# A 32-byte tile at SBUF's upper end in a retention and two-FFN kernel

## The chip, the cores and the metric

The kernel runs on one core of one Trainium2 chip. The metric is the device time of one execution in microseconds (us); the time of a kernel is the median of its runs. Times of single pieces come from one profiled execution.

## What is computed

A retention layer (linear attention with a decayed state) is followed by two feed-forward layers on 3072 tokens of width 512. All inputs are float32.

```python
# q, k, v: (4, 8, 768, 64)
state = gamma * state + k[t] (x) v[t]          # per head, 64 x 64
y[t] = scale * q[t] @ state
x = y as (3072, 512)
x = leaky_relu(x @ moe_w_in) @ moe_w_out       # 512 -> 2048 -> 512, slope 0.01
h = x @ moe2_w_in                              # 512 -> 2048
out = (h * sigmoid(1.702 * h)) @ moe2_w_out    # 2048 -> 512
```

## The kernel before

The work has three parts, and TensorE is the engine on which they follow each other.

**Numbers as two halves.** A float32 operand is split into a high part, rounded to TensorE's `float32r` type, and a low part, the remainder (`split`, lines 122 to 124). A product then takes three matmuls: high by low, high by high, low by high. So every large matmul here multiplies a stationary 128x128 block (the weights, `lhsT`) with a moving block of 128 rows and 512 or 384 columns (`rhs`), both of 4-byte numbers.

**First part: retention and the first FFN.** 24 steps of retention are interleaved with the first FFN. `ffn_in` (line 202) computes `h<-xs,home`: 12 matmuls of 512 columns for each of 16 slices of the hidden width and 6 blocks of 512 tokens. `ffn_out` (line 484) computes `y<-g,home`: 12 matmuls of 512 columns for each of the same slices. Weights come as 64-bit numbers and are converted by `work` on ScalarE, VectorE and GpSimd (lines 137 to 150) before their first use; those of `w_out` are converted while the first token block runs through `ffn_out`. Between them the weights of the second FFN are prepared (`Prep`).

**Second part: x times w_in of the second FFN.** `first` works in Strassen's scheme with 7 products (line 574): six matmuls of 384 columns for each product, `a`, `b` and `c<-xf,home`. The gated result goes to the DRAM tensor `gd`.

**Third part: times w_out of the second FFN.** `second` also has 7 products (line 757): matmuls of 512 columns, `d`, `e`, `f` and `h<-op,home`, in chains of 48. The blocks come back from `gd`, are combined (line 735) and split into `op` (lines 708 and 713). Line 769 transposes results with an identity matrix, `ident`.

**Where tiles lie.** Each tile belongs to a pool, and each pool grows from one of two sides of SBUF. The pools "left" are stacked upwards from the lower end, the pools "right" downwards from the upper end:

```python
pool = lambda c, name, bufs, side: c.enter_context(
    tc.tile_pool(name=name, bufs=bufs, side=side, reuse_waits="tile"))
homes = lambda n: pool(ctx, f"home{n}", 1, "left").tile([P, 4 * WQ], F32R, name=f"home{n}")
rest = {kind: pool(low, "rest" + kind, 1, "right").tile([P, 2048], F32R, name="rest" + kind) for kind in "io"}
g_p, h_p = pool(low, "g", 2, "right"), pool(low, "h", KF - 1, "right")
x_p, xs_p = pool(low_x, "x", 1, "right"), pool(low_x, "xs", 1, "right")
```

The lower side holds the weights of 14 of the 16 slices (`home0`, `home1`), the retention's tiles, and in the second part `xr`, `xt`, `xf`, `p`, `sg` and `g`. The upper side holds `resti` and `resto` (the weights of the last two slices of each matrix), `g`, `h`, `x`, `xs` and the conversion's `raw` and `a` in the first part, and in the third `op`, `ident`, `u` and the blocks of `gd`. In the built program the upper side's first tile, `resti`, begins at byte 221152 of a partition, and all other tiles of that side a multiple of 64 bytes below it: 221152 is 32 more than a multiple of 64. `home0` begins at 16512, `home1` at 73856 and the `xf` tiles at 146560 and so on, which are multiples of 64.

So the moving operands of lines 202, 484 and 757 (`xs`, `g`, `op`) begin 32 bytes past a multiple of 64, those of line 574 (`xf`) at a multiple; the stationary operands begin at a multiple except for `resti` and `resto`.

Of the kernel before, what the change touches and what calls it, by code (L numbers as in the profile page):

```python
# [9 lines left out]
F32 = mybir.dt.float32  # L10
# [9 lines left out]
P = 128  # L20
# [63 lines left out]
def retention_two_ffn(ctx: ExitStack, tc: tile.TileContext, qkv, consts, small, w1i, w1o, w2i, w2o, scratch, out):  # L84
# [5 lines left out]
    pool = lambda c, name, bufs, side: c.enter_context(  # L90
        tc.tile_pool(name=name, bufs=bufs, side=side, reuse_waits="tile"))
    homes = lambda n: pool(ctx, f"home{n}", 1, "left").tile([P, 4 * WQ], F32R, name=f"home{n}")
    low, low_x = ExitStack(), ExitStack()
    home = {"i": homes(0)}
    rest = {kind: pool(low, "rest" + kind, 1, "right").tile([P, 2048], F32R, name="rest" + kind) for kind in "io"}

# [433 lines left out]
    left, right = ExitStack(), ExitStack()  # L530
# [386 lines left out]
```

## Time and profile before

| what | value |
|---|---|
| median of the three runs shown | 1142.4 us |
| all three runs | 1141.04, 1142.4, 2821.34 us |
| the profiled execution | 1140.88 us |
| its span, first to last instruction | 1139.1 us |
| mean granted TensorE clock | 0.995 |
| TensorE's matmuls busy | 1115.6 us (98%) |
| VectorE busy | 694.6 us (61%) |
| ScalarE busy | 492.3 us (43%) |
| GpSimd busy | 269.1 us (24%) |
| DMA, mean over the span | 175 GB/s |

The busy time of an engine is the union of its instructions' times. Matmuls overlap: each takes some 400 ns from start to end, and the next starts about 233 ns after it, so the mean duration of one is not what it costs. What a matmul costs is the distance of two starts, read from a chain of them.

### The profile page before, as it was taken

The numbers are of one execution on the slowest core, as the hardware profiler recorded it, in microseconds if no ns is written. First come the engines' busy times: TensorE is split into PE (matmuls) and PEld (weight loads), VectorE is DVE, ScalarE is ACT, GpSimd is POOL, SyncE is SP. The second block draws the span as 40 slices with busy tenths as digits, with TensorE's granted clock in tenths as the row PEclk, the third lists the DMA queues.
The fourth block names the chain that finished last, engine by engine and source line by source line (L and its number), as shares of the span: only waits on it lengthen the run. The fifth ranks groups of instructions, "written<-read, shape, count | busy, mean of one in ns | idle before, by whom it ended". The sixth has DMA issues, their size and how long they took to land.

```text
span 1139.1 us, 16412 instructions
## 1 busy us (share of the span) xinstructions
PE 1115.6 (98%) x6188; PEld 939.2 (82%) x6189; DVE 694.6 (61%) x1034; ACT 492.3 (43%) x823; POOL 269.1 (24%) x269
## 2 busy tenths in 40 slices
PE   8999989999999999999999999999998999999997
PEld 5888867788888888888888899999998788888886
DVE  5977669645455546455442547575654686786774
ACT  2544445444344444344342434353432444545543
POOL 3655346422324233233321111111100000000000
PEclk9999989999999999999999999999999999999999
DMA  9888433225354445353449633436289625326322
GB/s 365 315 330 304 170 138 115 78 81 172 120 182 153 145 156 173 118 173 126 129 155 422 232 125 111 167 111 238 101 280 371 240 75 191 105 75 203 107 61 74
DMA packets 88095, 199.03 MB, mean 175 GB/s; under 512 B 7888, under 2 KB 51920, under 8 KB 82640
## 3 DMA queue, kind: packets, MB, share of 16 engines
q1 hardware_dynamic: 69584, 172.81, 43.6%
q10 hardware_dynamic: 18432, 25.17, 6.1%
q8 instruction: 48, 0.79, 0.3%
q14 instruction: 31, 0.25, 0.1%
HBM read 125.60 MB, written 72.35 MB: 174 GB/s over the span
## 4 chain that ended last, share of the span: by engine, by line
PE 92%; DMA 3%; DVE 2%; issue 1%; POOL 0%; ACT 0%; SPq 0%; ACTq 0%; POOLq 0%; DVEq 0%
PE h L202 23%; PE y L484 22%; PE b L574 9%; PE e L757 6%; PE d L757 6%; PE f L757 6%; PE a L574 6%; PE c L574 6%; PE h L757 3%; PE s L250 2%; PE o L287 2%; PE o L293 2%; DMA in<-qkv 1%; PE kv L281 1%; PE y L769 1%
## 5 line engine op out<-in xcount | busy, mean ns | idle before, releaser
L484 PE MATMUL y<-g,home 128*128 128x512 f32 x1008 | 250.0, 398 | 6.1 <-ACT home L123 3.7
L202 PE MATMUL h<-xs,home 128*128 128x512 f32 x1008 | 251.1, 397 | 0.0
L484 PEld LDWEIGHTS y<-g,home 128*128 128x128 f32 x1008 | 190.1, 189 | 54.5 <-POOL home L124 4.5
L202 PEld LDWEIGHTS h<-xs,home 128*128 128x128 f32 x1008 | 188.7, 188 | 47.4 <-issue 2.2
L124 DVE TENSOR_TENSOR g<-h,g 128x512 fp32r<-128x512 f32 x96 | 100.8, 1050 | 162.5 <-ACT g L123 162.5
L708 ACT CAST op<-g 128x512 fp32r<-128x512 f32 x168 | 100.9, 621 | 93.8 <-DVE g L735 42.1
L713 DVE TENSOR_TENSOR op<-g,op 128x512 fp32r<-128x512 f32 x168 | 112.1, 685 | 42.4 <-ACT op L708 39.8
L207 ACT ACTIVATE h<-h 128x512 f32<-128x512 f32 x96 | 57.3, 597 | 176.1 <-PE h L202 173.9
L574 PE MATMUL b<-xf,home 128*128 128x384 f32 x576 | 115.3, 334 | 1.2 <-DVE g L604 0.7
L574 PEld LDWEIGHTS b<-xf,home 128*128 128x128 f32 x576 | 101.1, 188 | 1.8 <-DVE g L604 1.0
L402 POOL TENSOR_TENSOR f<-f,raw 128x512 int32<-128x512 int32 x32 | 41.7, 1305 | 254.8 <-DVE f L398 254.8
L123 ACT CAST g<-h 128x512 fp32r<-128x512 f32 x96 | 59.7, 621 | 86.3 <-PE y L484 86.2
L574 PE MATMUL a<-xf,home 128*128 128x384 f32 x384 | 76.8, 334 | 0.0
L574 PE MATMUL c<-xf,home 128*128 128x384 f32 x384 | 76.8, 334 | 0.0
L757 PE MATMUL d<-op,home 128*128 128x512 f32 x288 | 70.3, 402 | 5.6 <-DVE op L713 5.6
L735 DVE TENSOR_TENSOR g<-g 128x512 f32<-128x512 f32 x96 | 72.1, 751 | 3.0 <-DMA g<-gd 3.0
L408 POOL TENSOR_TENSOR f<-f 128x128 f32<-128x128 f32 x128 | 71.9, 581 | 5.0
L757 PEld LDWEIGHTS d<-op,home 128*128 128x128 f32 x288 | 54.9, 192 | 19.2 <-DVE op L713 6.0
L757 PE MATMUL e<-op,home 128*128 128x512 f32 x288 | 70.2, 398 | 0.0
L757 PE MATMUL f<-op,home 128*128 128x512 f32 x288 | 68.2, 395 | 0.0
L574 PEld LDWEIGHTS a<-xf,home 128*128 128x128 f32 x384 | 67.5, 188 | 0.1
L574 PEld LDWEIGHTS c<-xf,home 128*128 128x128 f32 x384 | 67.5, 188 | 0.0
(94 smaller groups left out, 1396.7 us busy)
## 6 DMA issues: line engine op xcount, KB each, us to landing
gd<-g ACTq DMA_DIRECT2D x128, 192.0 KB, 2.0
g<-gd SPq DMA_DIRECT2D x96, 256.0 KB, 4.6
in<-qkv SPq DMA_DIRECT2D x21, 1024.0 KB, 7.1
home<-wdi SPq DMA_DIRECT2D x8, 1792.0 KB, 12.9
home<-wdo SPq DMA_DIRECT2D x8, 1792.0 KB, 9.6
raw<-w1i SPq DMA_DIRECT2D x16, 512.0 KB, 5.5
raw<-w1o SPq DMA_DIRECT2D x16, 512.0 KB, 3.3
raw<-w2i SPq DMA_DIRECT2D x32, 256.0 KB, 3.8
```

The lines of the kernel that those rows point to most:

```text
L123: nc.scalar.copy(out=hi, in_=src)
L124: (eng or nc.vector).tensor_tensor(out=lo, in0=src, in1=hi.bitcast(F32), op=ALU.subtract)
L202: nc.tensor.matmul(out=h, lhsT=w[:, a, k], rhs=xs[k][:, c], start=(i == 0), stop=(i == 3 * NP - 1))
L207: nc.scalar.activation(out=t, in_=h, func=AF.Lrelu)
L402: nc.gpsimd.tensor_tensor(out=self.f.bitcast(I32), in0=self.f.bitcast(I32), in1=self.low.bitcast(I32), op=ALU.add)
L408: nc.gpsimd.tensor_tensor(out=f[:, o], in0=f[:, a], in1=f[:, b], op=ALU.subtract)
L484: nc.tensor.matmul(out=y[j], lhsT=w[:, a, j * P : j * P + P], rhs=g[:, c], start=(m == 0 and i == 0), stop=(m == KF - 1 and i == 2))
L574: nc.tensor.matmul(out=t, lhsT=w[:, k, a], rhs=x[:, b, k], start=(start and m == 0), stop=(m == 5), skip_group_check=True)
L708: nc.scalar.copy(out=t[:, 0], in_=block_of(raw, *item))
L713: nc.vector.tensor_tensor(out=t[:, 1], in0=block_of(raw, *item), in1=t[:, 0].bitcast(F32), op=ALU.subtract)
L735: nc.vector.tensor_tensor(out=a(*s[0]), in0=a(*s[1]), in1=a(*s[2]), op=s[3])
L757: nc.tensor.matmul(out=t[:, j], lhsT=w[:, j, a], rhs=x[:, b], start=(new and q == 0 and m == 0), stop=(q == NQ - 1 and m == 2), skip_group ...
```

## The change

One line opens a pool of its own on the right, before all other pools of that side, with one tile of 8 float32 numbers (32 bytes in each partition). Nothing writes or reads it. It stays open to the end.

```diff
     low, low_x = ExitStack(), ExitStack()
+
+    pool(ctx, "pad", 1, "right").tile([P, 8], F32, name="pad")
     home = {"i": homes(0)}
     rest = {kind: pool(low, "rest" + kind, 1, "right").tile([P, 2048], F32R, name="rest" + kind) for kind in "io"}
```

In the built program each tile of the right side lies 32 bytes lower (`resti` at 221120, `xs` at 149440 for 149472, `op` at 225216 for 225248 and so on), at a multiple of 64. Tiles of the left side stay. The instructions of every engine, their order, their shapes and the semaphores that they wait for are the same as before; line numbers after line 93 are higher by two.

## Rows read from the trace of the kernel before

**Rows 1.** The page's first part: busy us of each engine, share, instructions.
```profile
PE 1115.6 (98%) x6188; PEld 939.2 (82%) x6189; DVE 694.6 (61%) x1034; ACT 492.3 (43%) x823; POOL 269.1 (24%) x269
```

**Rows 2.** Stretches: length, busy us by engine (instructions), granted TensorE clock, DMA share, GB/s.
```profile
30.00:143.00 113.00, 113.00 (x1300) 91.17 (x1297) 86.78 (x138) 50.95 (x88) 61.02 (x46) 1.00 0.78 279
149.40:153.70 4.30, 4.30 (x12) 3.33 (x11) 3.23 (x4) 1.98 (x5) 2.94 (x3) 0.50 0.39 122
157.00:205.00 48.00, 46.25 (x195) 36.02 (x194) 44.23 (x51) 28.20 (x48) 30.86 (x21) 1.00 0.33 108
215.00:645.00 430.00, 430.00 (x1851) 346.88 (x1850) 208.00 (x275) 179.52 (x284) 123.51 (x166) 1.00 0.48 166
650.00:873.00 223.00, 222.54 (x1284) 222.54 (x1285) 133.55 (x238) 88.17 (x176) 22.56 (x12) 1.00 0.52 182
889.00:1131.00 242.00, 242.00 (x1083) 195.35 (x1082) 176.55 (x266) 116.11 (x183) 8.18 (x3) 1.00 0.37 121
```

**Rows 3.** TensorE's longest waits: who waited for whom, us in total, times, longest.
```profile
PE d L757 <- DVE op L713: 5.6, 1, 5.6
PE y L484 <- ACT home L123: 3.7, 1, 3.7
PE y L484 <- POOL home L124: 2.4, 5, 0.6
```

**Rows 4.** The chain that ended last, from 299 us: start, us, engine, line, matmuls.
```profile
299.64 2.80 PE y L484 x12
302.44 2.80 PE h L202 x12
305.24 2.77 PE y L484 x12
308.00 2.80 PE h L202 x12
```

**Rows 5.** Groups of matmuls from 215 to 645 us: operands, shapes, count | busy, mean ns.
```profile
L484 PE MATMUL y<-g,home 128*128 128x512 f32 x840 | 206.0, 395 | 0.0
L202 PE MATMUL h<-xs,home 128*128 128x512 f32 x736 | 181.7, 395 | 0.0
L484 PE MATMUL y<-g,resto 128*128 128x512 f32 x144 | 34.9, 392 | 0.0
L202 PE MATMUL h<-xs,resti 128*128 128x512 f32 x120 | 29.3, 393 | 0.0
```

**Rows 6.** The chain that ended last, in the second part (384 columns).
```profile
661.32 1.04 PE c L574 x6
662.36 1.04 PE b L574 x6
```

**Rows 7.** The chain that ended last, in the third part (512 columns).
```profile
897.09 11.20 PE e L757 x48
908.29 11.20 PE f L757 x48
```

**Rows 8.** TensorE's instructions in order of time, 148 to 157 us: start, us, count.
```profile
148.80 4.63 PE L484 MATMUL y<-g,home 128*128 128x512 f32 x10 [0.61 <-POOL home L124]
153.24 3.73 PE L202 MATMUL h<-xs,home 128*128 128x512 f32 x12
```

**Rows 9.** Waits from 157 to 205 us: who waited for whom, us in total, times, longest.
```profile
PE y L484 <- POOL home L124: 1.8, 4, 0.5
```

**Rows 10.** Groups of VectorE and ScalarE: output<-input, shapes, count | busy, mean ns.
```profile
L713 DVE TENSOR_TENSOR op<-g,op 128x512 fp32r<-128x512 f32 x168 | 112.1, 685 | 42.4 <-ACT op L708 39.8 <-DMA g<-gd 1.4
L469 DVE TENSOR_TENSOR xf<-xr,xf 128x768 fp32r<-128x768 f32 x16 | 15.2, 952 | 2.8 <-ACT xf L468 2.4
L708 ACT CAST op<-g 128x512 fp32r<-128x512 f32 x168 | 100.9, 621 | 93.8 <-DVE g L735 42.1 <-PE f L757 15.6 <-PE e L757 13.3
L468 ACT CAST xf<-xr 128x768 fp32r<-128x768 f32 x16 | 13.3, 832 | 2.3 <-DMA xd<-y 2.3
```

**Rows 11.** The chain that ended last, at 1040 us: eight transposes.
```profile
1040.41 0.87 PE y L769 x8
```

## The prediction

> **What bounds the kernel now.** I read the busy times first: TensorE's matmuls fill 98% of the span, the next engine, VectorE, 61% [rows 1]. An average hides stages, so the stretches come next [rows 2]: from 215 to 645 us and from 889 to 1131 us TensorE is busy all the time, and no other engine above 73% there (VectorE, 176.55 of 242 us); from 157 to 205 us VectorE is at 44.23 of 48 us and TensorE is the one that now and then waits. Then the waits of TensorE: few and single, 5.6 us at the start of the third part, 3.7 us before the first `y` matmul, five of at most 0.6 us [rows 3]. So time can only come out of the matmuls themselves, and the question is what one of them costs by its start address, since the change alters nothing else.
>
> The chain of waits shows that cost as the distance of starts. A block of 12 matmuls of 512 columns with weights from `home0` or `home1` takes 2.80 us, 233.3 ns each [rows 4]; 48 in the third part take 11.20 us, again 233.3 ns [rows 7]. Six matmuls of 384 columns take 1.04 us, 173.3 ns each [rows 6]. The granted clock is 1.00 in all these stretches [rows 2], the level of 2.4 GHz, at which 512 columns take 213.3 ns and 384 take 160.0 ns at one column a cycle. What is over that is 20.0 ns for 512 columns and 13.3 ns for 384.
>
> Three things speak for the moving operand's start address as a part of it. First, the 384-column ones read tiles of the left side, at multiples of 64 bytes, and the 512-column ones read tiles 32 bytes off; the difference of the two excesses, 6.67 ns, is the time of 16 columns, which is 64 bytes of the moving stream. 2048 bytes that begin 32 bytes off a multiple of 64 touch 33 pieces of 64 bytes instead of 32; 1536 bytes that begin at a multiple touch just 24. Both stages then cost two pieces over the number touched. Second, the addresses of the weights matter: the block whose weights lie in `resto`, 32 bytes off like its moving operand, takes 2.77 us instead of 2.80 [rows 4], 230.8 ns each by the rounded row. Third, at half the clock the excess is gone: in 149.4 to 153.7 us, after a wait of 3.7 us for a converted weight [rows 3], the granted clock is 0.50 (1.2 GHz) [rows 2], and the matmuls there run at about one column a cycle: ten of them take 4.44 us from their first start to that of the next block [rows 8], 444 ns each with one delayed start among them, where 512 columns at 1.2 GHz take 426.7 ns. A cost of decoding or of the array would not vanish; a memory that delivers at a fixed rate, just short at 2.4 GHz, would behave so.
>
> **The change part by part.** The unused tile issues nothing: no instruction, no DMA, no wait, cost 0. All instructions, their order and what they wait for stay; 32 bytes of free space go. What is left is the address of each right-side tile.
>
> *Matmuls at lines 202, 484 and 757.* They would cost what the left-side form costs over its columns, 13.3 ns: 226.7 ns instead of 233.3, 6.67 ns less (233.3 - 226.7). The trace does not show an aligned operand of 512 columns, so the bounds: from above 233.3, as now (and 3 ns over it, see the rival on the slower side); from below 213.3, the bare column time. I take 226.7, the row with 4-byte operands at multiples of 64. By stretch:
> - 215 to 645 us: 840 + 736 = 1576 matmuls with `home` weights [rows 5], 1576 x 6.67 = 10.5 us. Those with `resto` and `resti`, 144 + 120 = 264, are at 2.77/12 = 230.8 ns now, 4.1 ns over 226.7: 264 x 4.1 = 1.1 us. VectorE has 208 of 430 us busy there, so nothing takes the place of the matmuls.
> - 889 to 1131 us: 1083 instructions less 88 transposes are 995 matmuls, x 6.67 = 6.6 us. VectorE at 176.55 of 242 us still fits in 235.
> - Before 143 us: 192 matmuls of line 202, 168 with `home` (x 6.67) and 24 with `resti` (x 4.1), 1.2 us. TensorE is busy throughout from 30 us, and the DMA engines are at 0.78 [rows 2], so loads can follow a stage that is 1% shorter. If they can't, this term is 0.
> - 149.4 to 157 us, at 1.2 GHz: 0, since no excess is seen there.
> - 157 to 205 us: TensorE waits four times for converted weights, 1.8 us in total [rows 9], with VectorE at 92%. A faster TensorE only waits longer, so its 195 matmuls (195 x 6.67 = 1.3 us) count as 0; if the conversion has slack after all, the 1.3 us come on top. The 44 matmuls or so of 205 to 215 us, without waits, give 0.3 us.
>
> *The second part, 650 to 873 us:* everything that its matmuls read is on the left side: 0.
>
> *Transposes (line 769):* eight take 0.87 us [rows 11], 109 ns each for 128 columns, twice the 53 ns of their columns, so the moving stream is not what they wait for. Their data move too; I count 0, with bounds of 6.67 ns either way for each of 96, 0.6 us.
>
> *VectorE, ScalarE, GpSimd.* Compare a right-side group with a left-side one of the same kind: VectorE's subtraction takes 685 ns for 512 columns on the right and 952 ns for 768 on the left [rows 10]. The 256 columns between them cost 267 ns, 1.04 ns a column, which leaves 685 - 533 = 152 and 952 - 800 = 152 ns. ScalarE: 621 and 832 ns, 0.82 ns a column, and 199 ns left over in both. No trace of the address: 0; and they lie beside TensorE except from 157 to 205 us. The DMAs into these tiles are the same in number and size; the one place where TensorE waits for their result, the 5.6 us at the start of the third part [rows 3], would have to shrink by a third to give 2 us, and I count 0.
>
> Sum: 10.5 + 1.1 + 6.6 + 1.2 + 0.3 = 19.7 us. The profiled execution took 1140.9 us (1139.1 in the span, 1.8 around it), 0.1% under the median of 1142.4, so I put the forecast against it: 1140.9 - 19.7 = 1121.2 us, 1.7% less. A difference of 2% is about what a measurement of this kernel can tell from no change, and this one stays just inside.
>
> A rule of the Trainium skill speaks against it. "SBUF — State Buffer", section "Door 1: The DMA port swizzle (why `[64,N]` ≈ `[32,N]`)", gives SBUF lines of 16 bytes, with a penalty where accesses cross to a new line. 32 is a multiple of 16, so by that rule the old addresses already begin on a line, both layouts touch the same number of lines, and the sum would be 0. The trace does not fit it well: the two kinds of block in [rows 4] differ only in whether the weights begin at a multiple of 64 or 32 past it, and take different times. A second rule, in "TensorE: Matmul & The Clock Gate", section "Step-by-step: what each phase is for", says that two independent read ports keep the next weights from slowing the running matmul; by that the 2.77 and the 2.80 us blocks would be equal, which they are not.
>
> **The rivals.**
>
> *Nothing happens (start addresses in steps of 32 bytes are free).* Mechanism: the moving stream is fetched in pieces of 32 bytes or fewer, of which it touches the same number before and after, and the 20.0 and 13.3 ns differ by the number of columns (for instance 6.67 ns for each 128 columns after the first). It is what the Trainium skill's rule of 16-byte lines on the page above would make of this kernel. For it: I have no row with equal columns and different alignment of the moving operand. Against it: the `resto` blocks, where an address of 32 bytes off moves the time. Time: 1141 us.
>
> *The excess goes with the columns, and alignment gives back a part.* 13.3 ns x 512/384 = 17.8 ns, 2.2 ns less than now, 2.2/6.67 of the sum: 6.5 us, 1134.4 us. For it: two points fit a line as well as a step. Against it: 2.2 ns is no multiple of anything seen.
>
> *More is gained.* If the left-side excess of 13.3 ns is due to the weights and the moving stream meeting unequally spread over the shorter matmul, a longer aligned stream may hide half of it: 6.67 ns more on some 2800 matmuls, 18.7 us, 1102.5 us. For it: excess vanishes at half the clock, so it is no fixed cost. Against it: 173.3 ns holds over the whole second part, with weights and moving operand both at multiples of 64.
>
> *Slower: the streams collide.* With weights and moving operand on the same grid of 64 bytes, each fetch of weights may fall on the fetch of the moving stream, as it cannot while the two are half a piece apart. Place: every matmul of lines 202, 484 and 757. Price: if what the `resto` blocks gain by their weights' address (233.3 - 230.8 = 2.5 ns) were lost instead, 3300 x 2.5 = 8 us, 1149 us; it decides from any distance above 233.3 ns. Against it: in `resto` blocks both are on the same grid and faster, and the same holds in the second part.
>
> **How the numbers follow.** The forecast, 1121.2 us with a range of its own from 1117 (the 1.3, the 0.6 and some of the waits come on top) to 1125 (the early stage and the `resto` share give nothing): 0.66. Nothing happens: 0.15. Part of it: 0.07. More: 0.08. Slower: 0.04. Outside 1116 to 1143 us lie most of the third and the last of the rivals, about 0.12. Faster by over 2% means under 1119 or so: the rival with more (0.08) and the lower end of the forecast (0.14), 0.22. Slower by over 2% needs 1165 us, 0.01. Within 2%: 0.77.
>
> **What would show it right or wrong.** In the chain of waits of the changed kernel, 12 matmuls of lines 204 and 486 would stand with 2.72 us, whatever their weights, and 48 of line 759 with 10.88 us; six of line 576 with 1.04 us as before. The stretch of 430 us would be 418 us long, the third part 6.6 us shorter, and the waits for converted weights around 157 to 205 us would each be some 0.2 us longer. Blocks of 2.80 us would refute the step on the matmuls outright; 2.77 us would say that only the agreement of weights and moving operand counts. If the blocks shrink but the span does not, a wait has opened that I did not see, and it would stand before a `y` matmul for `g` or before a `d` matmul for `op`.

## The result and the profile after

The changed kernel takes 1128.7 us in the median (1126.96 to 1129.34), 1141.8 us before; the ratio is 0.989 with a 95% interval of 0.9876 to 0.9904. One of the four runs before took 2821.34 us; the ratio leaves it out, and without it their median is 1141.2 us. The kernel is faster, and by less than 2%, as forecast. The size does not hold: 19.7 us less was forecast (1121.2 us), and the profiled execution went from 1140.88 to 1128.83 us, 12.05 us less. 1128.7 lies outside the forecast's own range of 1117 to 1125 us; it lies inside 1116 to 1143 us only because that range also covers the rivals, one of which is that nothing happens. A part of the mechanism must be wrong.

The page's first part of the changed kernel answers to [rows 1]: TensorE lost 12.3 us of busy time, the other engines changed by 1.8 us at most.

```profile
PE 1103.3 (98%) x6188; PEld 940.3 (83%) x6189; DVE 696.4 (62%) x1034; ACT 491.5 (44%) x823; POOL 269.8 (24%) x269
```

The chain that ended last in the changed kernel (start, us, engine, line, matmuls) answers to [rows 4, 6, 7]; lines are two higher.

```profile
299.97 2.75 PE h L204 x12
302.72 2.72 PE y L486 x12
...
660.98 1.04 PE b L576 x6
...
888.90 10.99 PE e L759 x48
```

Blocks with `home` weights fell from 2.80 to 2.75 us, chains of 48 from 11.20 to 10.99 us: 229.0 ns a matmul, not the 226.7 forecast. The block with `resto` weights (at 302.72) has the forecast's 2.72 us, 226.7 ns. The 384-column ones stay at 173.3 ns. So two kinds of block still differ although every start address of these matmuls is now a multiple of 64.

The stretches (columns as in [rows 2]) show that the rest is nearly as it was: the clock, VectorE's load, the DMA share, and half the clock after the wait before the first `y` matmul.

```profile
149.20:153.00 3.80, 3.80 (x10) 2.97 (x9) 3.22 (x4) 1.78 (x4) 2.44 (x3) 0.50 0.45 138
156.00:204.00 48.00, 45.59 (x195) 36.05 (x193) 45.06 (x51) 28.00 (x47) 31.74 (x21) 1.00 0.33 112
212.00:636.00 424.00, 424.00 (x1858) 348.62 (x1857) 210.65 (x276) 179.60 (x286) 125.72 (x167) 1.00 0.48 169
```

From 156 to 204 us the same 195 matmuls take the same 48 us with 0.66 us less busy time than in [rows 2]: the gain turned into waiting. TensorE's longest waits, to set beside [rows 3]:

```profile
PE d L759 <- DVE op L715: 5.7, 1, 5.7
PE y L486 <- ACT home L125: 3.8, 1, 3.8
PE y L486 <- POOL home L126: 2.7, 5, 0.7
PE b L576 <- DVE g L606: 1.4, 1, 1.4
```

The last of these waits was there before, too, but shorter:

```profile
PE b L574 <- DVE g L604: 0.7, 1, 0.7
```

The instructions and their order are the same in both kernels, so the start of one and the same matmul can be set side by side, which shows where the time went:

| start of the same matmul | before, us | after, us | us gained since the row above |
|---|---|---|---|
| `y`, the first of ten that run on, at half the clock | 148.80 | 148.62 | 0.18 (since the start) |
| `y` after the next `h` block, at the full clock | 156.80 | 156.03 | 0.59 |
| `y` after the last wait for a converted weight | 204.79 | 204.13 | -0.11 |
| the first of line 574 (576) | 643.23 | 634.42 | 8.15 |
| `d` after the wait at the start of the third part | 885.62 | 877.71 | -0.90 |
| the last group of transposes | 1132.91 | 1120.83 | 4.17 |

The 0.59 us in the second row are mostly a matter of the clock: before, the granted clock is still 0.50 from 154.0 to 154.6 us, and with the change it is 0.91 from 153.4 to 154.0 us. What brought it back some 1 us sooner is not shown.

### The profile page after: what moved, and what is told of

Same layout as the page of the kernel before. It is cut to its first block, busy times and chain, and to the rows that moved or that the text cites. A ratio compares the mean times of both kernels' runs of the same rounds, so it can differ in the third digit from the quotient of the medians.

```text
span 1127.0 us, 16412 instructions
## 1 busy us (share of the span) xinstructions
PE 1103.3 (98%) x6188; PEld 940.3 (83%) x6189; DVE 696.4 (62%) x1034; ACT 491.5 (44%) x823; POOL 269.8 (24%) x269
## 4 chain that ended last, share of the span: by engine, by line
PE 91%; DVE 4%; DMA 2%; issue 1%; ACT 1%; POOL 0%; SPq 0%; ACTq 0%; DVEq 0%; POOLq 0%
PE h L204 22%; PE y L486 22%; PE b L576 9%; PE a L576 6%; PE d L759 6%; PE f L759 6%; PE c L576 6%; PE e L759 5%; PE h L759 3%; PE s L252 2%; PE o L289 2%; PE o L295 2%; PE kv L283 1%; DMA home<-wdo 1%; DVE raw L141 1%
## 5 line engine op out<-in xcount | busy, mean ns | idle before, releaser
L486 PE MATMUL y<-g,home 128*128 128x512 f32 x1008 | 246.2, 395 | 6.5 <-ACT home L125 3.8
L204 PE MATMUL h<-xs,home 128*128 128x512 f32 x1008 | 246.5, 394 | 0.0
```

The lines of the kernel that those rows point to most:

```text
L204: nc.tensor.matmul(out=h, lhsT=w[:, a, k], rhs=xs[k][:, c], start=(i == 0), stop=(i == 3 * NP - 1))
L486: nc.tensor.matmul(out=y[j], lhsT=w[:, a, j * P : j * P + P], rhs=g[:, c], start=(m == 0 and i == 0), stop=(m == KF - 1 and i == 2))
```

## The experiments

**Three theories.** Only addresses changed, so the question is which property of them counts. *Theory G* is the prediction's: each operand by itself, whether it begins at a multiple of 64 bytes. *Theory M*: the moving operand's own start, modulo 128. *Theory D*: the distance of the moving operand from the weights, `moving - home`, modulo some period, whatever the two are by themselves. The last came from the blocks above: `resto` lies at the same place modulo 128 as `g`, and `home` does not. Addresses below are those of the built programs; a distance is given modulo 256 bytes, between `xs`, `g` or `op` and `home0` or `home1`. It was 96 before the change and is 64 with it. Between `xf` and the `home` weights it is 0 in both kernels, and so it is between `xs` and `resti` and between `g` and `resto`.

One thing fits no theory of a block's own distance: `resto` blocks have distance 0 in both kernels, and yet take 2.77 us before [rows 4] and 2.72 with the change. Inside such a block of the kernel before, the first seven matmuls take 1.62 us, 231 ns each, and then three take 0.68 us, 226.7 ns each:

```profile
305.24 1.62 PE y L484 x7
306.86 0.68 PE y L484 x3
```

So a block also depends on the one that ran before it. This comes back with the weights that are 16 bytes into their tiles.

**The tile of 96 bytes instead of 32 (right96), distance 0.**

```diff
-    pool(ctx, "pad", 1, "right").tile([P, 8], F32, name="pad")
+    pool(ctx, "pad", 1, "right").tile([P, 24], F32, name="pad")
```

> The unused tile has 96 bytes for 32: right-side tiles begin at multiples of 128 (the change: 64 past one), home weights at multiples of 128 as always. Theory D (the distance of moving operand and weights modulo 128 sets the cost, 0 is best): all 512-column matmuls at 226.7 ns, 12 of them in 2.72 us for 2.75 with the change, 48 in 10.88 us; 3024 x 2.28 = 6.9 us less than the change, about 1122 us. Theory M (the moving operand's own start modulo 128 sets it, 0 is best): the same. Theory G (only multiples of 64 count, for each operand by itself): 2.75 us stays, 1128.7 us.

Measured: 1122.76 us, ratio to the kernel before the change 0.9839 (0.9825 to 0.9854). Its chain:

```profile
297.52 2.72 PE h L204 x12
300.24 2.72 PE y L486 x12
...
665.13 1.04 PE c L576 x6
...
895.15 10.88 PE f L759 x48
```

All blocks are at 226.7 ns. Theory G alone has fallen: with all starts at multiples of 64, as with the change and here, there are still two speeds.

**Both sides 64 past a multiple of 128 (right32_left64), distance 0.**

```diff
     pool(ctx, "pad", 1, "right").tile([P, 8], F32, name="pad")
+    pool(ctx, "padl", 1, "left").tile([P, 16], F32, name="padl")
```

> The change, and an unused tile of 64 bytes at the lower end too: both sides begin 64 past a multiple of 128, so the distance is 0 and no start is at a multiple of 128. Theory D: 226.7 ns, 12 in 2.72 us, 48 in 10.88 us, six of 384 columns in 1.04 us as before, about 1122 us. Theory M: 229.0 ns as with the change, 12 in 2.75 us, and the 384-column matmuls slower than 173.3 ns by up to 2.3 ns, 1129 to 1132 us. Theory G: as the change, 1128.7 us.

Measured: 1122.31 us, ratio 0.9835 (0.9818 to 0.9851).

```profile
300.61 2.72 PE y L487 x12
...
665.14 1.04 PE c L577 x6
...
906.07 10.88 PE d L760 x48
```

The moving operands lie where they do with the change, and yet a block takes 2.72 us: theory M has fallen, and it is the weights' place beside theirs that did it.

**No operand of the large matmuls at a multiple of 64 (left96), distance 0.**

```diff
-    pool(ctx, "pad", 1, "right").tile([P, 8], F32, name="pad")
+    pool(ctx, "padl", 1, "left").tile([P, 24], F32, name="padl")
```

> No tile at the upper end but one of 96 bytes at the lower end: both sides begin 96 past a multiple of 128, so the distance is 0 and nothing is at a multiple of 64. Theory D: 226.7 ns, 12 in 2.72 us, 48 in 10.88 us, six of 384 columns in 1.04 us, about 1122 us. Theory M: 233.3 ns as before the change, and the 384-column matmuls some 5 ns slower, 1141 + 1344 x 5 ns = 1148 us. Theory G: 233.3 ns and 180 ns, 1141 + 1344 x 6.7 ns = 1150 us.

Measured: 1123.51 us, ratio 0.9842 (0.9827 to 0.9857).

```profile
298.00 2.72 PE h L204 x12
300.71 2.72 PE y L486 x12
...
665.96 1.04 PE c L576 x6
...
896.83 10.88 PE f L759 x48
```

This settles it against alignment. The right side is untouched, each moving operand of the first and third part begins 32 bytes off a multiple of 64 as before, `xf` and the weights do so now as well, and the whole gain is there, with 173.3 ns for 384 columns still. Of the three theories only the distance is left.

**A control (right64), distance 32.** The tile has 64 bytes (`[P, 16]`).

> A control: the unused tile at the upper end has 64 bytes, so right-side tiles begin 32 past a multiple of 128 (before the change: 96 past it), still 32 off a multiple of 64. Theory D: a distance of 32 for one of 96, both a quarter of the period off, so 233.3 ns, 12 in 2.80 us, 1141 us. Theories M and G: 233.3 ns too, 1141 us. If a shift of any size helps, the time falls as with the change to 1129 us.

Measured: 1140.8 us, ratio 0.9996 (0.9985 to 1.0007). A shift alone gives nothing: the chain shows `home` blocks as before, and `resto`, which still agrees with `g`, faster (2.73 us).

```profile
300.63 2.79 PE h L204 x12
303.43 2.73 PE y L486 x12
...
896.22 11.20 PE e L759 x48
```

**The period (right224), distance 128.** The tile has 224 bytes (`[P, 56]`), so that the right side begins at multiples of 128, of 256 even.

> The unused tile has 224 bytes: right-side tiles are again at multiples of 128, but the distance of moving operand and weights is 128 modulo 256, where with 96 bytes it is 0. Theory D with a period of 128 bytes: 226.7 ns, 12 in 2.72 us, 1122 to 1123 us as with 96 bytes. Theory D with a period of 256 or more: a distance of 128 costs something, as 64 does (229.0 ns, 12 in 2.75 us) or more, 1129 us or above.

Measured: 1138.93 us, ratio 0.9975 (0.9965 to 0.9985).

```profile
298.08 2.79 PE y L486 x12
300.87 2.78 PE h L204 x12
303.66 2.73 PE y L486 x12
...
895.04 11.16 PE e L759 x48
```

A period of 128 has fallen: at 128 a matmul costs 232.5 ns. Nor is the period 512: modulo 512 the three kernels of distance 0 are at 256 (`xs` less `home0`), while the `rest` tiles are at 0, and both reach 226.7 ns.

**The direction (right160), distance 192.** The tile has 160 bytes (`[P, 40]`).

> The unused tile has 160 bytes: the distance is -64 bytes (192 modulo 256) where the change has 64. If only the size of the distance counts: 229.0 ns, 12 in 2.75 us, 48 in 10.99 us, 1128 to 1129 us. If its direction counts (weights ahead of or behind the moving stream): another value between 226.7 and 233.4 ns, 1122 to 1141 us.

Measured: 1140.99 us, ratio 0.9995 (0.9986 to 1.0005).

```profile
298.55 2.80 PE y L486 x12
301.35 2.80 PE h L204 x12
304.14 2.75 PE y L486 x12
...
897.27 11.20 PE e L759 x48
```

A moving operand 64 bytes ahead of the weights modulo 256 cost 229.0 ns, 64 behind 233.3 ns: the direction counts. The `resto` block (at 304.14), at distance 0 as in every kernel so far, takes 2.75 us here, 2.73 in right64 and in the block shown of right224, 2.72 with the change and 2.77 before: its time goes with the blocks around it.

**Weights 16 bytes into their tiles (right96_home16).**

The tile of 96 bytes is there as in right96; to the kernel before, the edit is (some lines between are left out):

```diff
-    homes = lambda n: pool(ctx, f"home{n}", 1, "left").tile([P, 4 * WQ], F32R, name=f"home{n}")
+    homes = lambda n: pool(ctx, f"home{n}", 1, "left").tile([P, 4 * WQ + 32], F32R, name=f"home{n}")[:, 4 : 4 * WQ + 4]
...
+    pool(ctx, "pad", 1, "right").tile([P, 24], F32, name="pad")
```

> As with 96 bytes at the upper end, but the weights of home0 and home1 begin 16 bytes into their tiles, so the distance is 16 bytes for every matmul with home weights, the 384-column ones too, while resti and resto keep 0. Theory D has no value for 16: if any distance counts, between 226.7 (distance 0) and over 233.3 ns (32), 12 in 2.72 to 2.82 us, and the 384-column ones above 173.3 ns; if the grain is 32 bytes, 226.7 or 233.3 ns sharp. By the rule that 16-byte lines are all that counts, distance 32 could not have cost anything, and 16 would cost nothing either: 1122 us. My guess is about 230 ns, with 175 ns for 384 columns, 1122 + 3024 x 3.3 ns + 1344 x 2 ns = 1135 us.

Measured: 1129.78 us, ratio 0.9891 (0.9878 to 0.9905). The experiment is not quite the one announced: the larger `home0` pushes `home1` up by 128 bytes, so the distance is 240 with `home0` and 112 with `home1`. So it tries two other distances instead of 16; the guess of 1135 us was 5 us too high. What it showed was not expected by any theory. The chain around 214 us, where the first block of distance 0 after the waits for converted weights runs (`y` with `resto` weights), and pieces of the second and third part:

```profile
208.14 2.81 PE y L486 x12
210.95 2.80 PE h L204 x12
213.75 2.75 PE y L486 x12
216.49 2.72 PE h L204 x12
...
646.31 1.06 PE a L576 x6
...
676.75 1.04 PE b L576 x6
...
898.62 10.88 PE f L759 x48
...
948.50 8.16 PE h L759 x36
...
960.25 8.40 PE d L759 x36
...
979.86 11.20 PE f L759 x48
```

`h` blocks at 210.95 and 216.49 us are the same work at the same distance, 2.80 us before the `resto` block and 2.72 us after it, and it stays so to the end of the first part. (Two `resti` blocks of distance 0 had run earlier, among the retention's steps; after the waits that followed them, blocks took 2.80 us.) In the third part the first block of tokens runs at 10.88 us for 48, the second at 11.20, with the same two distances (half of each chain reads `home0`, half `home1`). So the distance does not set the cost by itself: there is a state that lasts from one matmul to the next. That it is a phase between the two streams which TensorE reads is an explanation and not shown; "phase" stands for it below. In the second part no such state is seen: blocks of 384 columns take 1.06 us (176.7 ns) where the weights come from `home0` and 1.04 us (173.3 ns) where they come from `home1`, all through.

**The same without a block of distance 0 in the first FFN (right96_all16).** `resti` and `resto` get the same 16 bytes (`[P, 2048 + 32]`, sliced from 4).

> As the kernel with weights 16 bytes into home0 and home1, but resti and resto are moved by 16 bytes too (their tiles grow by 128 bytes each), so that no block of the first FFN has a distance of 0: modulo 256 it is 240 with home0, 112 with home1, resti and resto. In the kernel before this one the first FFN went from 2.80 us a block to 2.72 us at the first resto block, whose distance was 0, and stayed there with the same home weights. Theory H (the streams keep the phase that they have; a block of distance 0 brings it in order, and a distance of 16 does not disturb it): without such a block 2.80 us stays to the end of the first part, and the time is about 1140 us. Theory D alone (the distance of a block sets its cost): the blocks with home weights are as there, 2.72 us from 214 us on, 1130 us.

In the built program `resto` is at 240 and only `home1` and `resti` at 112; no block of the first FFN is at 0, as intended.

Measured: 1142.77 us, ratio 1.0013 (1.0004 to 1.0023).

```profile
211.87 2.80 PE h L204 x12
214.67 2.80 PE y L486 x12
...
980.75 11.20 PE e L759 x48
...
1062.66 10.88 PE e L759 x48
```

Without that block 2.80 us stays to the end of the first part, as theory H says and theory D alone does not. The third part goes the other way round than in right96_home16: slow in its first two blocks of tokens, fast in the last. In both kernels each change of speed in the third part falls on a group of transposes or on a wait, where the run of 512-column matmuls is broken off (as between 948.50 and 960.25 us in the chain above). Why the speed is high after one of them and low after another was not found.

**Moving the retention's tiles as well (right96_smalls).** With the tile of 96 bytes, `smalls` is 24 numbers longer and the tiles behind it begin at multiples of 128.

> As with 96 bytes at the upper end, and the retention's smalls tile is 96 bytes longer, so that the tiles behind it (cst, st, sm, qs) begin at multiples of 128 like the tile in; before they are 32 off. Of the retention's matmuls only those of line 289 (weights sm, moving in, or the reverse) change their distance, from 32 to 0. Theory D: the 16 matmuls of a step there take less than 0.88 us, by at most 16 x 6.7 ns = 0.1 us, some 2 us in 24 steps, 1120 to 1122 us. If 128-column matmuls are not short of their moving stream, nothing: 1122.8 us.

Measured: 1124.3 us, ratio 0.9843 (0.9828 to 0.9858). The step's 16 matmuls, in the kernel before (line 287) and here (line 289):

```profile
24.98 0.88 PE o L287 x16
63.24 0.88 PE o L289 x16
```

They take 0.88 us as before, and the kernel is no faster than with the 96 bytes alone. But the expectation was written for a period of 128. Modulo 256, in the built program, the distance of these matmuls (`sm` from `in`) went from 32 to 128 and not to 0. So the run shows that this move gains them nothing; what distance 0 would do for matmuls of 128 columns is not shown.

**The change once more (change_again)**, on one chip with right224, right96_home16 and right96_smalls.

> The change itself, on the same chip as the others of this group. All theories: 12 matmuls with home weights in 2.75 us, with resto weights in 2.72 us, a time of 1127 to 1129 us, 5 to 7 us above the kernel with 224 bytes if the period is 128 bytes.

Measured: 1129.21 us, ratio 0.9886 (0.9871 to 0.9901).

```profile
299.02 2.75 PE h L204 x12
301.77 2.72 PE y L486 x12
...
889.98 10.99 PE e L759 x48
```

The block times are those of the first run of the change.

The kernels with one distance for all `home` weights together, with the cost of a 512-column matmul from the chains of 48 (us divided by 48); the two kernels with weights 16 bytes into their tiles have two distances and two speeds and are left out:

| distance modulo 256 | kernel | ns per matmul | median, us |
|---|---|---|---|
| 0 | right96, right32_left64, left96 | 226.7 | 1122.8, 1122.3, 1123.5 |
| 32 | right64 | 233.3 | 1140.8 |
| 64 | the change, change_again | 229.0 | 1128.7, 1129.2 |
| 96 | before | 233.3 | 1141.8 |
| 128 | right224 | 232.5 | 1138.9 |
| 192 | right160 | 233.3 | 1141.0 |

## Why the prediction was right in direction and wrong in mechanism and size

*What bounds the kernel: right.* The gain came out of TensorE's matmuls (12.3 us of busy time for 12.05 us of execution), and no other engine took over.

*The step that failed* is that matmuls at lines 202, 484 and 757 "would cost what the left-side form costs over its columns, 13.3 ns: 226.7 ns". The runs showed 229.0 ns in its place. The value 226.7 is real, but multiples of 64 do not give it; the right distance does. The pieces of 64 bytes, 33 or 32 of them, were a story that fitted three rows: left96 touches 33 in every moving operand of 512 columns and runs at 226.7 ns. That the time fell at all was luck in part: a move by 32 bytes made the distance 64 for 96, and moves by 64 or 160 bytes, which bring it to 32 and 192, give nothing. The prediction had the hint in hand, `resto` blocks faster through the weights' address alone, and even named "only the agreement of weights and moving operand counts" with a block time of its own (2.77 us), but did not price it as a rival.

*The terms, sized anew* with 233.3 - 229.0 = 4.4 ns (11.20 less 10.99 us, over 48):
- 215 to 645 us, `home` weights: 1576 x 4.4 = 6.9 us instead of 10.5.
- `resto` and `resti`: 2.72 us a block as forecast, 1.1 us, but not because their start moved to a multiple of 64: their distance was 0 before and after, and what changed is the blocks around them.
- 205 to 215 us: 0.2 us instead of 0.3. With the two terms above that is 8.2 us from 205 to 643 us, and 8.15 were measured.
- The third part: 995 x 4.4 = 4.4 us instead of 6.6; 4.17 were measured.
- Before 143 us: at the same rate 0.8 us instead of 1.2; only 0.2 were measured up to 148.8 us, and why is not shown.
- 149.4 to 157 us, put at 0: 0.6 us were gained, mostly since the clock came back sooner, which no address explains here.
- 157 to 205 us: 0, right; the gain became waiting.
- The second part, put at 0: 0.9 us were lost up to the third part's first matmuls. 0.7 of it is a wait that the prediction did not see: the last but one group of line 576 waits 1.4 us for `g` (line 606), where it was 0.7 us before. It is 1.1 us in right64, where the matmuls are as slow as before, so it also varies without the gain.

The measured pieces, 0.18 + 0.59 - 0.11 + 8.15 - 0.90 + 4.17, give the 12.1 us by which the span is shorter (1139.1 us before, 1127.0 after).

*The other terms put at 0: right.* The pad costs nothing; line 576 stays at 1.04 us a block. Transposes stay at 0.87 us for eight; both of their operands lie on the right side and move together. VectorE's subtraction into `op` takes 686 ns after 685, ScalarE's rounding 621 ns as before. The prediction's own argument for that (152 and 152 ns left over, 199 and 199) could not have come out otherwise: the rate per column came from the same two durations that it was then taken off, so the remainders had to be equal. The excess that is gone at half the clock is seen again: ten `y` matmuls take 4.44 us from 148.62 us to the start of the next block, as before, one late start among them; the others start 426 to 427 ns apart.

*The rivals.* "Nothing happens" is refuted for a shift of 32 bytes and would have been the truth for a shift of 64 or 160. "Alignment gives back a part" came nearest in time (1134.4 us), by another mechanism. "The streams collide" names the two operands that count, but has the wrong sign: at distance 0 they are fastest.

*The two rules of the Trainium skill.* By "SBUF — State Buffer", section "Door 1: The DMA port swizzle (why `[64,N]` ≈ `[32,N]`)", lines are 16 bytes, so a shift of 32 bytes would change nothing by it; here one is worth up to 6.6 ns a matmul (right64 to right96). By "TensorE: Matmul & The Clock Gate", section "Step-by-step: what each phase is for", loading the next weights takes no SBUF read bandwidth from the running matmul; left96 moves the weights and not the moving operand of the first and third part, and 233.3 ns become 226.7. Where page and trace differ, the trace decides.

*A version that beats both:* 96 bytes for 32, one number in the same line, 1122.8 us against 1128.7 with the change. In its group of runs it is some 18 us under the kernel before.

## What to carry to other kernels

Where TensorE multiplies 4-byte operands back to back, compare the time from one start to the next with columns over clock, block by block: an excess that differs between blocks of one shape was here a matter of addresses. Then look at the two operands' places against each other, not at each one's alignment; of the six distances in the table one was best, and an unused tile of the right size, on either side, set it. Read single blocks from several places of the trace, since a block's speed can depend on what ran before it. A hint that a term of the sum rests on (one block of another speed) deserves a rival and a price of its own.

## What the hardware showed that was not expected

- With 4-byte operands a matmul of 512 columns took 226.7 to 233.3 ns by the distance of its moving operand from the weights modulo 256 bytes, and at 1.2 GHz (granted clock 0.50) 426 to 427 ns, one column a cycle, without such an excess. That the two read streams of TensorE meet in SBUF's memory would explain both; it is argued, not shown. The table's values hold for runs of blocks at one distance.
- The phase lasts. At distances 240 and 112 the same blocks ran at 2.80 or 2.72 us, and one block of distance 0 turned the one into the other for the rest of the first part (from 214 us on in right96_home16, not in right96_all16). In the third part both speeds are seen without such a block, and they change at transposes and waits.
- A difference of the same size in the other direction is not the same: 64 costs 229.0 ns, 192 costs 233.3 ns.
